# Summing two of four kv batches on another engine, one load for four rows, third buffers, and a planner rule that starts late

## The chip, the cores and the metric

The kernel runs on one core of a Trainium2 chip. A core has TensorE (PE, matmuls), VectorE (DVE), ScalarE (ACT), GpSimd (POOL) and SyncE (SP, which issues most DMAs). The metric is the device time of one execution in microseconds (us).

## The reference

Two layers follow each other. The first is attention with pooled keys; the second a mixture of experts that sends each row to one expert.

```
kv_pool = kv.reshape(4, 96, 4, 8, 4, 128).mean(axis=(2, 4))      # 4 x 4 windows
k = v = kv_pool.reshape(4, 768, 128) @ w_sr
a = softmax(q @ k.T / sqrt(128))                                 # q: 4 x 12288 x 128
x = (a @ v).reshape(49152, 128)
logits = (x / |x|) @ (expert_emb / |expert_emb|).T / tau         # 8 experts
e = argmax(logits); g = softmax(logits)[e]
out[rows of e] = g * (relu(x[rows of e] @ w1[e]) @ w2[e])         # hidden width 1024
```

All inputs and the output are fp32. The kernel computes its large products in fp16 with two halves per number (a rounded high half and the low half that remains), so each product is three matmuls.

## The kernel before, in words

The rows of q are taken in 96 steps of 512 (24 for each batch). A step loads q, scales it, turns it (by PE up to step 28, from step 29 on by a transposing DMA out of a tile q2 that holds both halves, `q_hi`, `q_lo`, `q_turn`), multiplies it with the batch's k into four tiles of 128 x 768 scores (`s_mm`, line 684), takes the row maximum on DVE (`s_max`, line 689) and the exponential on ACT (`s_exp`, line 707). The result p is split into halves phi and plo (`p_hi` on ACT, line 725; `p_lo`, line 735, a subtraction on DVE or POOL), a transposing DMA turns each half (`p_t`, line 759), and PE multiplies with v (`av`, line 780). Some early steps turn p by PE instead (`p_turn`, `p_copy`). After four steps a group of 2048 rows is complete: some 18 small DVE operations make its logits (`g_logits`, lines 839 to 911), ranks and places follow, and POOL scatters the rows into expert order (line 188).

From step 23 on, expert tiles of 512 rows run beside the steps: three matmuls per unit (`l1`, line 1397), relu on ACT (`h_hi`, line 1404), the remainder on DVE (`h_lo`, line 1409), the second product (line 1433), the gate's multiply on DVE (`o_out`, line 1443) and scatters of the output on POOL. The expert weights are split into halves once, in the first stage, with a subtraction on POOL for 14 of 16 (`w_lo`, line 1048), and written to a buffer in DRAM. The expert tiles' buffers come from a pool `wk2`, which is opened when the first stage's pool is closed (`open_experts`).

The pooling of kv is done batch by batch, half a batch ahead. Batch 0 is summed by DVE at the start (`kv_load_0` and what follows). Each of the batches 1 to 3 has 8 windows h of 512 columns; for each, `kv_load` brings four rows of 96 x 512 numbers in two DMAs of 384 KB (line 381), each into one of two buffers `kvt`. POOL adds them in five operations: two rows and two rows (line 390), both sums (line 394), then the four columns in two steps (`kv_cols`, lines 406 and 411), into `pooled`. `kv_t`, `kv_k` and what follows turn the sums and make k and v.

The order of every engine's instructions is not written out: a planner (`Plan`) simulates the engines. Each operation has an engine, an estimated duration, a key (a planned time that serves as its priority), and what it depends on, buffers included: `turn(tag, n)` names the users of the buffer n uses back. In each turn the planner lets the engine that is free first take the ready operation of the lowest key. Operations marked `port=True` have one more rule: one on DVE is not begun while one on POOL is planned to run, nor the reverse. Another ready operation without the mark goes first, or the engine waits. The order that comes out is the order in each engine's queue; on the chip each engine works through its queue in order and waits on semaphores.

The parts that the change touches are: `kv_load`, `kv_rows`, `kv_cols` (lines 379 to 415) and their calls in `kv_ops` (lines 1518 to 1538), the port rule in `Plan.run` (line 295), the buffers of `q2` (line 649), `phi` (line 722) and `plo` (line 732) with their `turn` calls in `step_ops`, and the planned duration of the logits' operations in `group_ops`. A third buffer lets an operation start before the DMA that reads the buffer of two uses ago has landed.

Of the kernel before, what the change touches and what calls it, by code (L numbers as in the profile page):

```python
# [46 lines left out]
    avd=0.262, m=1.928, end=-1.35, ne=-6.946, ge=-32,  # L47
# [4 lines left out]
def attention_moe(  # L52
# [11 lines left out]
    nc = tc.nc  # L64
# [31 lines left out]
    PTB = 4  # L96
    NP = 6
# [119 lines left out]
    class Plan:  # L217
# [33 lines left out]
        def run(self, begin):  # L251
# [18 lines left out]
            while any(count):  # L270
# [24 lines left out]
                if op.port:  # L295
                    other = held["POOL" if eng == "DVE" else "DVE"]
                    if other > t + 0.1:
                        rest = [x for x in now[eng] if not x[2].port and self.can_go(x[2])]
                        if rest:
                            x = min(rest)  # L300
                            now[eng].remove(x)
                            now[eng].append((op.key, i, op))
                            heapq.heapify(now[eng])
                            op = x[2]
                        else:
                            t = other
# [70 lines left out]
    def kv_load(b, h, i):  # L377

        t = kvs.tile([NI, 2, QC], F32, tag="kvt", name=f"kvt{b}_{h}_{i}", bufs=2)
        src = kv[b].rearrange("(i r) w c -> i r (w c)", r=R)  # L380
        nc.sync.dma_start(out=t, in_=src[:, 2 * i : 2 * i + 2, h * QC : (h + 1) * QC])
        st[b]["kvt", h, i] = t

    def kv_rows(b, h, eng):


        def half(i):
            t = st[b].pop(("kvt", h, i))
            st[b]["r", h, i] = kvs.tile([NI, QC], F32, tag=f"kva{i}", name=f"kva{b}_{h}_{i}", bufs=2)
            eng.tensor_tensor(out=st[b]["r", h, i], in0=t[:, 0, :], in1=t[:, 1, :], op=ALU.add)  # L390

        def both():
            r = st[b]["r", h, 0]
            eng.tensor_tensor(out=r, in0=r, in1=st[b].pop(("r", h, 1)), op=ALU.add)

        return [lambda: half(0), lambda: half(1), both]

    def kv_cols(b, h, eng):


        def third():
            if h == 0:
                st[b]["pooled"] = kvs.tile([NI, NJ, C], F32, tag="pooled", name=f"pooled{b}")
            v = st[b].pop(("r", h, 0)).rearrange("p (j r c) -> p j r c", j=JQ, r=R)
            a3 = kvs.tile([NI, JQ, 2, C], F32, tag="kva3", name=f"kvc{b}_{h}", bufs=2)
            eng.tensor_tensor(out=a3, in0=v[:, :, 0:2, :], in1=v[:, :, 2:4, :], op=ALU.add)
            st[b]["a", h] = a3

        def fourth():
            a3 = st[b].pop(("a", h))  # L410
            eng.tensor_tensor(
                out=st[b]["pooled"][:, h * JQ : (h + 1) * JQ, :], in0=a3[:, :, 0, :], in1=a3[:, :, 1, :],
                op=ALU.add,
            )

        return [third, fourth]
# [230 lines left out]
    def q_hi(k):  # L647
        if by_dma(k):
            ks[k]["q2"] = wk.tile([P, NQ, 2, C], F16, tag="q2", name=f"q2_{k}")
# [69 lines left out]
    def p_hi(k, j):  # L719
        h, i = divmod(j, 2)  # L720
        if i == 0:
            ks[k]["h", h] = [wk.tile([P, 2, NK], F16, tag="phi", name=f"phi{k}_{h}")]
# [6 lines left out]
    def p_lo(k, j):  # L729
        h, i = divmod(j, 2)  # L730
        if i == 0:
            ks[k]["h", h].append(wk.tile([P, 2, NK], F16, tag="plo", name=f"plo{k}_{h}"))
# [785 lines left out]
    def kv_ops(b):  # L1518
        mine = [None] * NQR
        for h in range(NQR if b else 0):  # L1520
            t0 = slot(b * SPB, -8 * (X["kv"] - h * X["kvs"]))
            eng, what, ta, tb_ = nc.gpsimd, "POOL", 1.25, 0.7
            rows = kv_rows(b, h, eng)
            parts = []
            for i in range(2):
                o = add("SP", 0.45, t0 + i, lambda h=h, i=i: kv_load(b, h, i), *turn("kvt", 2), dma=1.3, hold=True)
                took("kvt", o)
                r = took(f"kva{i}", add(what, ta, t0 + 8.0 + i * 0.1, rows[i], o, *parts, *turn(f"kva{i}", 2), port=True))
                reads("kvt", r)
                parts.append(r)  # L1530
            r = add(what, ta, t0 + 8.2, rows[2], *parts, port=True)
            reads("kva1", r)
            cols = kv_cols(b, h, eng)
            r = add(what, tb_, t0 + 8.3, cols[0], r, *(turn("pooled", 1) if h == 0 else mine[h - 1 : h]), port=True)
            if h == 0:
                took("pooled", r)
            reads("kva0", r)
            mine[h] = add(what, 0.45, t0 + 8.4, cols[1], r, port=True)
# [99 lines left out]
    x_swap = None  # L1638
    scaled_q = {}
# [3 lines left out]
    def step_ops(k):  # L1643
# [19 lines left out]
        if by_dma(k):  # L1663
            key -= X["ql"]
            hi = took("q2", add("ACT", 0.61, key, lambda: q_hi(k), qa, *turn("q2", 2)))
# [13 lines left out]
        for j in range(NQ):  # L1679
# [16 lines left out]
            if j % 2:  # L1696
# [14 lines left out]
                for i in range(2):  # L1711
                    on = p_mode(k, j - 1 + i)
                    his.append(
                        add(ENG[on[0]], P_HI[on[0]], v + i, lambda j=j, i=i: p_hi(k, j - 1 + i), t_s[k][j - 1 + i], *(his if i else turn("phi", 2)))
                    )
                    if i == 0:
# [4 lines left out]
                            *(los if i else turn("plo", 2)), port=True,  # L1721
# [53 lines left out]
    def group_ops(g, t):  # L1775
        if g == NGRP - 1:
# [3 lines left out]
            t, 0.3, ops, *counted[g], *placed.get(g - 1, ()), *placed.get(g - 2, ()), dur=0.22, port=True,  # L1780
# [61 lines left out]
    x_open = add("-", 0.0, TM[0] - 20.0, open_experts, *stores, *early, v_ready[0])  # L1842

# [77 lines left out]
```

## Time and profile before

| what | value |
|---|---|
| median of 3 runs | 2122.8 us (2112.49 to 2125.25) |
| the profiled execution's own time | 2116.39 us |
| its span, first to last instruction | 2114.4 us |
| mean granted TensorE clock | 0.982 |
| busy: PE, DVE, ACT, POOL | 1954.2 (92%), 1722.0 (81%), 1548.1 (73%), 1323.6 us (63%) |

A row of the profile by stretch gives the busy time of PE, of PE's weight loads, of DVE, ACT and POOL, each with its count of instructions, then the clock that PE was granted (1.00 is 2.4 GHz), and the DMA engines' share. In a timeline a row is the start, the duration, the engine, the line and the operation, its output and inputs; what stands in brackets is the time that the engine idled before it, and whose end ended that. An operation's duration includes time in which it has begun and is held up.

### The profile page before, as it was taken

Reading aid. Unit: us, or ns where it says so; the run is one execution under the profiler, and the core shown is the slowest. Engines: PE = TensorE matmul, PEld = TensorE weight load, DVE = VectorE, ACT = ScalarE, POOL = GpSimd, SP = SyncE. Lnnn points to the kernel's source line nnn. Section 1 sums busy time; section 2 is a strip of 40 time slices with the busy share of each in tenths; the row PEclk is TensorE's granted clock in tenths of the full one; section 3 lists DMA queues with packets and bytes.
Section 4 is the critical chain, followed back from the end, with each engine's and each line's share of the span. In section 5 each row is a group of like instructions: output and inputs, shape, how many; then the busy total and the mean of one; then the engine's idle time right before and its main releaser. Section 6 shows DMA issues by size and latency. Waiting matters only on the chain. (4 is left out here: it accounts for less than half of the span.)

```text
span 2114.4 us, 57446 instructions
## 1 busy us (share of the span) xinstructions
PE 1954.2 (92%) x21396; PEld 1502.7 (71%) x21396; DVE 1722.0 (81%) x3679; ACT 1548.1 (73%) x3256; POOL 1323.6 (63%) x1824
## 2 busy tenths in 40 slices
PE   3777888799999999999999999899999999999998
PEld 2556666567777777677777777677777777777797
DVE  7887788598889899789889888788888888766565
ACT  3886789578787878787787888788888887744443
POOL 1547544468777876577876675566576577567443
PEclk9998999999999999999999999999999999999999
DMA  8977445889898998979898988979888888623242
GB/s 245 205 195 183 124 109 124 182 167 164 165 167 160 190 178 159 209 138 178 169 179 141 167 163 149 190 146 160 147 165 143 156 160 139 119 61 82 57 92 78
DMA packets 844925, 322.64 MB, mean 153 GB/s; under 512 B 793042, under 2 KB 804443, under 8 KB 842848
## 3 DMA queue, kind: packets, MB, share of 16 engines
q1 hardware_dynamic: 817568, 264.13, 66.8%
q0 software_dynamic: 24704, 53.53, 9.7%
q8 instruction: 170, 2.79, 0.5%
q10 hardware_dynamic: 2368, 1.25, 0.2%
q14 instruction: 115, 0.94, 0.2%
HBM read 170.55 MB, written 64.50 MB: 111 GB/s over the span
## 5 line engine op out<-in xcount | busy, mean ns | idle before, releaser
L1409 DVE SCALAR_TENSOR_TENSOR hl<-ph,hh 128x512 f16<-128x512 f32 x740 | 506.8, 686 | 185.7 <-ACT hh L1404 178.3
L188 POOL DMA_INDIRECT out_dram<-o,m x388 | 411.1, 1060 | 325.7 <-DVE o L1443 112.0
L1404 ACT ACTIVATE hh<-ph 128x512 f16<-128x512 f32 x740 | 440.5, 595 | 237.8 <-PE ph L1397 178.8
L1397 PE MATMUL ph<-x,wbuf 128*128 128x512 f16 (+1 forms) x2328 | 600.1, 370 | 8.9 <-DVE hl L1409 6.6
L188 POOL DMA_INDIRECT xs_rows<-rows,pi x384 | 417.7, 1088 | 146.4 <-issue 110.9
L1433 PE MATMUL po<-wbuf,hh 128*128 128x128 f16 x5920 | 453.5, 220 | 30.1 <-DVE o L1443 14.7
L684 PE MATMUL s<-k,qT 128*128 128x512 f16 (+1 forms) x2304 | 442.9, 332 | 30.6 <-ACT p L707 23.1
L707 ACT ACTIVATE p<-s,nm,qa 128x768 f32<-128x768 f32 x384 | 379.9, 990 | 83.3 <-DVE nm L701 75.9
L1433 PEld LDWEIGHTS <-hh 128*128 128x128 f16 x6208 | 383.5, 98 | 52.7 <-issue 23.0
L689 DVE TENSOR_REDUCE nm<-s 128x1 f32<-128x768 f32 x384 | 364.1, 948 | 25.2 <-PE s L684 23.3
L735 DVE TENSOR_TENSOR plo<-p,phi 128x768 f16<-128x768 f32 x339 | 340.8, 1006 | 29.4 <-ACT phi L725 19.0
L684 PEld LDWEIGHTS <-qT 128*128 128x128 f16 x2304 | 219.4, 99 | 165.7 <-issue 44.9
L780 PE MATMUL xp<-v,pthi 128*128 128x137 f16 x4200 | 314.6, 225 | 13.8 <-DVE w L567 5.4
L1397 PEld LDWEIGHTS <-wbuf 128*128 128x128 f16 x2544 | 226.2, 98 | 127.7 <-issue 13.7
L780 PEld LDWEIGHTS <-pthi 128*128 128x128 f16 x4200 | 276.7, 98 | 50.9 <-issue 17.0
L1433 PEld LDWEIGHTS <-hl 128*128 128x128 f16 x3104 | 228.9, 98 | 111.2 <-issue 1.7
L725 ACT CAST phi<-p 128x768 f16<-128x768 f32 x345 | 287.2, 834 | 13.7 <-DMA pthi<-phi 9.3
L1433 PE MATMUL po<-wbuf,hl 128*128 128x128 f16 x2960 | 286.4, 219 | 0.0
L780 PE MATMUL xp<-v,ptlo 128*128 128x137 f16 x2100 | 188.7, 226 | 0.0
L780 PEld LDWEIGHTS <-ptlo 128*128 128x128 f16 x2100 | 143.5, 98 | 0.0
L813 POOL TENSOR_TENSOR rows<-x,rows 128x512 f16<-128x512 f32 x96 | 111.7, 1164 | 25.7 <-ACT rows L808 25.4
L828 ACT ACTIVATE junk<-x 128x128 f32<-128x128 f32 x384 | 116.7, 312 | 13.5 <-DVE x L801 13.5
(359 smaller groups left out, 2004.7 us busy)
## 6 DMA issues: line engine op xcount, KB each, us to landing
wbuf<-w_prep SPq DMA_DIRECT2D x106, 1026.0 KB
kvt<-in_kv_dram SPq DMA_DIRECT2D x64, 384.0 KB
q<-in_q_dram SPq DMA_DIRECT2D x96, 256.0 KB
wf<-in_moe_w_dram SPq DMA_DIRECT2D x16, 512.0 KB
out_dram<-o,m POOLq DMA_INDIRECT x388
xs_rows<-rows,pi POOLq DMA_INDIRECT x384
w_prep<-wo SPq DMA_DIRECT2D x8, 514.0 KB
w_prep<-wo SPq DMA_DIRECT2D x8, 512.0 KB
```

The costliest lines, as they stand in the source:

```text
L188: ins = nc.gpsimd.indirect_dma_start(out=dst[:, :], out_offset=bass.IndirectOffsetOnAxis(ap=idx, axis=0), in_=src, in_offset=None, bounds_ ...
L684: nc.tensor.matmul(t[:, lo:hi], qs[:, l, :], r[:, lo:hi], start=i == 0, stop=i == 2)
L689: V.tensor_reduce(out=nm, in_=ks[k]["s", j], axis=AX.X, op=ALU.max, negate=True)
L707: nc.scalar.activation(out=p, in_=ks[k].pop(("s", j)), func=AF.Exp, bias=ks[k].pop(("nm", j)), scale=ks[k]["fac"],)
L725: nc.scalar.copy(out=hi, in_=p)
L735: eng.tensor_tensor(out=lo, in0=ks[k].pop(("p", j)), in1=hi, op=ALU.subtract)
L780: nc.tensor.matmul(ks[k]["xp", h][:, i, :w], l[:, c, :], r[:, c, :w], start=n == 0, stop=n == len(terms) - 1)
L828: nc.scalar.activation(out=junk, in_=ks[k]["x"][:, j, 0:C], func=AF.Square, accum_out=groups[g]["ss"][:, i * NQ + j : i * NQ + j + 1],)
L1397: nc.tensor.matmul(ph[:, kk * n : (kk + 1) * n], wt[:, o + f : o + f + P], r, start=i == 0, stop=i == 2)
L1404: nc.scalar.activation(out=hh, in_=ts[t]["ph", u], func=AF.Relu)
L1409: V.scalar_tensor_tensor(out=hl, in0=ts[t].pop(("ph", u)), scalar=0.0, in1=ts[t]["hh", u], op0=ALU.max, op1=ALU.subtract)
L1433: nc.tensor.matmul(ts[t]["po"][:, j * C : (j + 1) * C], h[:, kk * n + j * P : kk * n + (j + 1) * P], wt[:, f : f + P], start=u == 0 and i ...
```

## The change

The windows of batches 2 and 3 are summed by DVE: two reductions per window, each over rows and columns at once (16 numbers, 512 bytes apart) for 64 of the 128 channels. Batch 1 stays with POOL, whose five adds now work in place in the loaded tile. One DMA of 768 KB loads the four rows of a window, again with two buffers. The port rule holds only from the planner's time 350 on. The halves phi and plo have three buffers each instead of two. The tile q2 has three buffers instead of two and lies in `wk2`, so its steps wait for `open_experts`. The planned duration of the logits' operations is 0.17 instead of 0.22 for groups 0 to 3.

```diff
-    avd=0.262, m=1.928, end=-1.35, ne=-6.946, ge=-32,
+    avd=0.262, m=1.928, end=-1.35, ne=-6.946, ge=-32, pt=350.0, kd=(2, 3),
...
+    PB = 3
+    Q2 = 3
...
-                if op.port:
+                if op.port and t > X["pt"]:
...
+    def kv_load(b, h):
+        t = kvs.tile([NI, R, QC], F32, tag="kvt", name=f"kvt{b}_{h}", bufs=2)
+        nc.sync.dma_start(
+            out=t, in_=kv[b].rearrange("(i r) w c -> i r (w c)", r=R)[:, :, h * QC : (h + 1) * QC]
+        )
+        st[b]["kvt", h] = t
...
+        return [
+            lambda: add(row(0), row(0), row(1)), lambda: add(row(2), row(2), row(3)),
+            lambda: add(row(0), row(0), row(2)), lambda: add(cols(0, 2), cols(0, 2), cols(2, 4)),
+            lambda: add(lambda: kv_pooled(b, h), cols(0, 1), cols(1, 2)),
+        ]
+
+    def kv_window(b, h, i):
+        if i == 0:
+            kv_pooled(b, h)
+        c = slice(i * C // 2, (i + 1) * C // 2)
+        V.tensor_reduce(
+            out=st[b]["pooled"][:, h, c], in_=st[b]["kvt", h].rearrange("p r (w c) -> p c r w", w=R)[:, c],
+            axis=AX.XY, op=ALU.add,
+        )
...
-            ks[k]["q2"] = wk.tile([P, NQ, 2, C], F16, tag="q2", name=f"q2_{k}")
+            ks[k]["q2"] = wk2.tile([P, NQ, 2, C], F16, tag="q2", name=f"q2_{k}", bufs=Q2)
...
-            ks[k]["h", h] = [wk.tile([P, 2, NK], F16, tag="phi", name=f"phi{k}_{h}")]
+            ks[k]["h", h] = [wk.tile([P, 2, NK], F16, tag="phi", name=f"phi{k}_{h}", bufs=PB)]
...
-            ks[k]["h", h].append(wk.tile([P, 2, NK], F16, tag="plo", name=f"plo{k}_{h}"))
+            ks[k]["h", h].append(wk.tile([P, 2, NK], F16, tag="plo", name=f"plo{k}_{h}", bufs=PB))
...
+            o = took("kvt", add("SP", 0.45, t0, lambda h=h: kv_load(b, h), *turn("kvt", 2), dma=2.6, hold=True))
+            deps = turn("pooled", 1) if h == 0 else mine[h - 1 : h]
+            r = None
+            if b in X["kd"]:
+                for i in range(2):
+                    r = add("DVE", 1.2, t0 + 8.0 + 0.2 * i, lambda h=h, i=i: kv_window(b, h, i), o, r, *deps)
+                    reads("kvt", r)
+            else:
+                for i, (fn, dur) in enumerate(zip(kv_adds(b, h), (1.25, 1.25, 1.25, 0.7, 0.45))):
+                    r = add("POOL", dur, t0 + 8.0 + 0.1 * i, fn, o, r, *deps, port=True)
+                    reads("kvt", r)
...
-            hi = took("q2", add("ACT", 0.61, key, lambda: q_hi(k), qa, *turn("q2", 2)))
+            hi = took("q2", add("ACT", 0.61, key, lambda: q_hi(k), qa, *turn("q2", Q2)))
+            opened.append(hi)
...
-            t, 0.3, ops, *counted[g], *placed.get(g - 1, ()), *placed.get(g - 2, ()), dur=0.22, port=True,
+            t, 0.3, ops, *counted[g], *placed.get(g - 1, ()), *placed.get(g - 2, ()), dur=0.22 if g > 3 else 0.17, port=True,
...
+    for o in opened:
+        o.left += 1
+        x_open.users.append(o)
```

## Rows read from the trace of the kernel before

**Rows 1.** Busy time of every engine by stretch: busy us (instructions), PEclk, DMA share, GB/s

```profile
45.00:130.00 85.00, 66.86 (x605) 50.19 (x604) 71.06 (x149) 70.65 (x142) 38.45 (x31) 0.94 0.85 196
...
130.00:260.00 130.00, 100.20 (x762) 80.95 (x762) 102.09 (x217) 91.29 (x184) 86.77 (x91) 0.88 0.68 171
...
260.00:400.00 140.00, 112.60 (x952) 88.22 (x951) 106.89 (x262) 107.77 (x229) 64.11 (x100) 0.94 0.55 124
...
400.00:450.00 50.00, 42.14 (x413) 29.91 (x413) 37.63 (x69) 31.11 (x69) 27.85 (x42) 0.97 0.88 186
...
450.00:1150.00 700.00, 676.44 (x7663) 513.59 (x7661) 619.29 (x1305) 554.90 (x1198) 516.90 (x720) 1.00 0.90 169
...
1150.00:1850.00 700.00, 691.03 (x7895) 527.62 (x7894) 597.53 (x1306) 563.36 (x1207) 451.91 (x652) 1.00 0.85 155
```

**Rows 2.** PE's waits from 450 to 1150 us: us in total, times, longest

```profile
PE po L1433 <- DVE o L1443: 8.7, 10, 3.0
...
PE po L1433 <- ACT hh L1404: 7.7, 6, 4.2
```

**Rows 3.** Timelines of DVE, POOL and PE: start, us, engine, line, operation [idle before]

```profile
429.22 3.05 DVE L851 TENSOR_TENSOR n4z<-y 128x16 f32<-128x16 f32 x1
...
429.74 2.49 POOL L390 TENSOR_TENSOR kva<-kvt 96x512 f32<-96x512 f32 x2
...
432.93 1.35 PE L1397 MATMUL ph<-x,wbuf 128*128 128x512 f16 x3 [2.15 <-DVE hl L1409]
...
643.42 3.79 DVE L618 TENSOR_SCALAR qa<-qa 128x2 int32<-128x2 int32 x1
...
643.49 2.48 POOL L390 TENSOR_TENSOR kva<-kvt 96x512 f32<-96x512 f32 x2
...
648.80 1.01 PE L1433 MATMUL po<-wbuf,hh 128*128 128x128 f16 x8 [2.97 <-DVE o L1443]
...
741.68 1.22 DVE L618 TENSOR_SCALAR qa<-qa 128x2 int32<-128x2 int32 x1
```

**Rows 4.** Timelines of ACT and PE around the late relu

```profile
859.09 0.72 ACT L650 ACTIVATE q<-q,qa 128x512 f16<-128x512 f32 x1 [3.99 <-DMA qT<-q]
...
860.35 1.03 PE L1433 MATMUL po<-wbuf,hh 128*128 128x128 f16 x8 [4.17 <-ACT hh L1404]
...
1355.19 1.03 PE L1433 MATMUL po<-wbuf,hh 128*128 128x128 f16 x8 [4.09 <-ACT hh L1404]
```

**Rows 5.** Groups by line, POOL, 400 to 1150 us: busy us, mean ns

```profile
L390 POOL TENSOR_TENSOR kva<-kvt 96x512 f32<-96x512 f32 x32 | 40.7, 1283 | 6.1 <-DMA kvt<-in_kv_dram 6.1
```

**Rows 6.** Single lines, whole run: ns min/median/max, first and last start

```profile
L1007 DVE TENSOR_REDUCE wm<-wf x16: 1196/1206/1219, 35.7 to 219.9; 128x1 f32<-128x1024 f32 x16
...
L650 ACT ACTIVATE q<-q,qa x67: 707/721/761, 453.9 to 1760.0; 128x512 f16<-128x512 f32 x67
...
L381 SPq DMA_DIRECT2D kvt<-in_kv_dram x48: 312/393/1195, 122.0 to 1070.3; - x48
```

**Rows 7.** Waits of all engines from 40 to 400 us

```profile
PE s L684 <- ACT p L707: 22.2, 20, 2.9
...
PE s L369 <- ACT p L707: 17.6, 16, 2.6
...
ACT phi L725 <- DMA pthi<-phi: 5.4, 1, 5.4
```

**Rows 8.** Timelines of DVE, POOL and PE in the first stage

```profile
129.44 4.45 DVE L854 SCALAR_TENSOR_TENSOR n0z<-n0z,ss 128x16 f32<-128x16 f32 x1
...
272.23 4.58 DVE L632 TENSOR_SCALAR qa<-qa,ksc 128x2 f32<-128x2 f32 x1
...
272.57 4.21 POOL L1048 TENSOR_TENSOR wo<-wf,wo 128x1024 f16<-128x1024 f32 x2
...
278.41 0.87 PE L369 MATMUL pp<-ident,pooled 96*128 96x96 f32 x4 [5.17 <-DVE nm L701]
```

**Rows 9.** Groups by line, POOL, 45 to 400 us

```profile
L188 POOL DMA_INDIRECT xs_rows<-rows,pi x56 | 59.6, 1065 | 23.6 <-issue 15.4 <-DVE rows L976 5.3 <-DVE nm L701 2.3
```

More of the change, by code (lines that the diff above doesn't have):

```diff
@@ L375, in attention_moe @@
     st = [dict() for _ in range(B)]
[L377 to L416, printed above, removed]
+    def kv_load(b, h):
[4 more added lines that the diff above has]
+        st[b]["kvt", h] = t
@@ new lines, in kv_pooled, with kv_adds, add, row @@
+    def kv_pooled(b, h):
+        if h == 0:
+            st[b]["pooled"] = kvs.tile([NI, NJ, C], F32, tag="pooled", name=f"pooled{b}")
+        return st[b]["pooled"][:, h, :]
+    def kv_adds(b, h):
+        def add(out, in0, in1):
+            nc.gpsimd.tensor_tensor(out=out(), in0=in0(), in1=in1(), op=ALU.add)
+        def row(i):
+            return lambda: st[b]["kvt", h][:, i, :]
+        def cols(lo, hi):
+            return lambda: st[b]["kvt", h][:, 0, lo * C : hi * C]
+        return [
[3 more added lines that the diff above has]
+        ]
@@ L1521, in kv_ops @@
             t0 = slot(b * SPB, -8 * (X["kv"] - h * X["kvs"]))
[L1522 to L1534, printed above, removed]
+            o = took("kvt", add("SP", 0.45, t0, lambda h=h: kv_load(b, h), *turn("kvt", 2), dma=2.6, hold=True))
[9 more added lines that the diff above has]
+                    reads("kvt", r)
             if h == 0:
                 took("pooled", r)
-            reads("kva0", r)
-            mine[h] = add(what, 0.45, t0 + 8.4, cols[1], r, port=True)
+            mine[h] = r
         copies = []
@@ L1638, in attention_moe @@
     x_swap = None
+    opened = []
     scaled_q = {}
@@ L1713, in step_ops @@
                     his.append(
-                        add(ENG[on[0]], P_HI[on[0]], v + i, lambda j=j, i=i: p_hi(k, j - 1 + i), t_s[k][j - 1 + i], *(his if i else turn("phi", 2)))
+                        add(ENG[on[0]], P_HI[on[0]], v + i, lambda j=j, i=i: p_hi(k, j - 1 + i), t_s[k][j - 1 + i], *(his if i else turn("phi", PB)))
                     )
@@ L1720, in step_ops @@
                             ENG[on[1]], P_LO[on[1]], v + i + 0.5, lambda j=j, i=i: p_lo(k, j - 1 + i), his[i],
-                            *(los if i else turn("plo", 2)), port=True,
+                            *(los if i else turn("plo", PB)), port=True,
                         )
```

## The prediction

> **What bounds the kernel now.** The busy times by stretch come first [rows 1]. The reader is to see three stages. From 45 to 400 us PE is busy 66.86 + 100.20 + 112.60 = 279.7 of 355 us at a granted clock of 0.88 to 0.94, and no other engine is near full either (DVE 280, ACT 270): this stage, the attention steps that run before any expert tile, is bound by waits between engines. From 450 to 1850 PE is busy over 96% at a clock of 1.00: PE is the bound, and only its idle time can be won. What comes after 1850 the change does not touch. So the change can take time away in two places: the 75 us that PE idles from 45 to 400, and the 7.9 + 23.6 + 9.0 us that it idles from 400 to 1850. A change that only lightens POOL or DVE is worth nothing by itself; it has to end a wait of PE.
>
> Next I read the two stretches of 700 us against each other [rows 1]. They do the same work per step, but the batch sums of batches 2 and 3 lie almost wholly in the first. There POOL is busy 65 us more, DVE 21.8 us more, and PE idles 23.6 instead of 9.0 us. The list of PE's waits in the first one says for whom: 8.7 us for DVE's last multiply of an expert tile, 7.7 us for ACT's relu [rows 2].
>
> Then the timeline around the longest of these [rows 3]. At 643.42 a DVE operation on no more than 128x2 numbers takes 3.79 us. It stands beside POOL adds of kv rows that run from 643.49 on, two in one row of the timeline and a third behind them, and ends with the third. Behind it in DVE's queue stands the multiply of an expert tile, and PE waits 2.97 us for that. At 429.22 a 128x16 operation takes 3.05 us beside two such adds, and PE waits 2.15 us. So a POOL add and a DVE operation that reads SBUF twice, or in its fast form, do not run together, and the loser holds up its whole queue. A block of 1.22 us, at 741.68, was followed by no wait of PE.
>
> The second kind of wait is at 860.35 and 1355.19 [rows 4]: PE waits 4.17 and 4.09 us for a relu, and in front of the first ACT waited 3.99 us in the scaling of q for a transposing DMA to release one of the two q2 buffers (the second is preceded by the same row, with 4.52 us).
>
> **The change, part by part.**
>
> *POOL's sums of batches 2 and 3 go.* The adds of single rows alone are 32 operations and 40.7 us [rows 5]; with the other three kinds POOL is busy the 65 us longer. POOL is no bound (517 of 700 us), so this is worth only what it blocked. The difference in PE's idle time between the two stretches is 14.6 us, and the wait at 432.93 lies ahead of them: 2.15 us. Together 16.7 us at most; at the least nothing, if each wait comes back elsewhere.
>
> *DVE's reductions come.* Two for each of 8 windows of two batches: 32, each reading 96 x 1024 numbers. The nearest row is the DVE reduction over 1024 numbers of SBUF, 1206 ns, with a spread of 1196 to 1219 over 16 of them, so nothing of POOL's held one up [rows 6]. I take 1.2 us: 32 x 1.2 = 38.4 us. DVE gets back about the 21.8 us that it is busy longer in the first stretch. So it goes from 619 to 636 of 700 us: fuller, but not the bound. Below 1.2 us one can hardly come, since that row reads as many numbers side by side; the trace has no wide stride of that size, and I bound it above by twice the row, 2.4 us. The reductions have late keys, so the planner lets them into gaps of DVE, but what comes ready during one waits for its end: relu remainders, maxima, the multiply of a tile. A block of 1.22 us cost PE nothing [rows 3]. I take 0.2 us of PE each, 6.4 us; at 2.4 us a block is close to those that cost PE 2 us, and I take 1 us each, 32 us, for the far end.
>
> *A third q2 buffer.* It ends the waits of 4.17 and 4.09 us, 8.3 us, if the DMA that is late is no later than a step; otherwise nothing. I take 8.3. Moving the tile into the pool that opens with the experts makes these steps wait for that opening; the first of them scales its q at 453.9 us [rows 6], when expert tiles already run (the wait at 432.93 is in one) [rows 3]. That costs nothing.
>
> *Third buffers for the split halves of p.* In the first stage ACT waits 5.4 us for a transposing DMA to give a buffer back [rows 7]. The ends for PE are 0 and 5.4 us; I take 3, because ACT's work is on the way to PE's waits for p there.
>
> *One load for four rows.* 24 issues of SP in place of 48, each 393 ns in the middle [rows 6]: 9.4 us less in SP's queue, where the transposing DMAs of p, q and x stand behind them. In return a load is twice as long and holds its buffer until the last add has read it. Both buffers now hold a whole window, so POOL's first add is less often late. From -2 to +2 us; I take 0.
>
> *The port rule from 350 on only.* Until then the planner orders DVE and POOL by key alone. Nothing on the chip changes by that, only the order of the queues. The rule's present worth can be seen in what still goes wrong: at 272.23 a DVE operation takes 4.58 us and PE waits 5.17 us behind it; at 129.44 one takes 4.45 us [rows 8]. POOL is busy 38.45 + 86.77 + 64.11 = 189.3 of 355 us there [rows 1], and without its scatters, 59.6 us [rows 9], 130 us, 37%. In that stage DVE has by the code some 170 operations that can collide: some 50 low halves of p, about 22 for each of four groups, and scalings of q and w. Met at random, each loses half a POOL operation (half of the 1.28 us of a kv add [rows 5] or of the 2.1 us of a weight's low half [rows 8], an estimated 0.8 us) in 37% of the cases: 170 x 0.37 x 0.8 = 50 us of DVE. Blocks like the two just named already hold a part of that, so the rule prevents a part, not all. Against it: without the rule no urgent operation is put behind a less urgent one, and 39.8 us of PE's waits here are for p from ACT, which hangs on DVE's maxima [rows 7]. The ends are -20 us (half of those waits) and +50 us (all collisions new, all passed on). I take 0.
>
> **The sum.** For 400 to 1850: -16.7 - 8.3 + 6.4 = -18.6, of which I count 15, since a tile that is no longer late for one reason is partly late for the next. With -3 for the buffers of p that is -18. The profiled execution took 2116.4 us (span 2114.4): 2116.4 - 18 = 2098. The median of the runs shown, 2122.8, is 6 us above that execution, and 2098 is 1.2% below the median. About 1%, 21 us, is what a measurement of this kernel can tell from no change.
>
> **The rivals.**
> A. The forecast: 2098, its own range 2086 to 2110.
> B. The first stage shortens too: the order by key alone brings p earlier, and half of PE's waits for it go. For it: no engine is full there, and 39.8 us of waits have one cause [rows 7]. Against it: the longest waits there are collisions, which it does not prevent. 2098 - 20 = 2078.
> C. The reductions are slow: reading numbers 512 bytes apart takes 2.4 us each, DVE is at 636 + 38 = 674 of 700 us, and PE pays 32 instead of 6 us. 2098 + 26 = 2124. For it: no row of before reads so. Against it: the planner is given 1.2 us.
> The Trainium skill speaks for C ("SBUF — State Buffer", section "Door 1: The DMA port swizzle (why [64,N] ≈ [32,N])", the note on cachelines): SBUF is read in lines of 16 bytes, and a read pattern that takes only one number of each line is slowed. By this rule the 32 reductions cost more than the row of contiguous reading; no run here shows it yet.
> D. The other side: without the rule the first stage collides more. Place: 45 to 400 us. Price: up to 50 us, and PE takes nearly all of a long block, as at 272.23 [rows 8]. It decides from the point where it eats the 18 us won: half the price gives 2123, the whole 2148; I take 2135. For it: two blocks of over 4 us stand there even with the rule [rows 8]. Against it: the planner's times there are wrong enough that the rule already misses most of what it is for.
> E. The waits are only moved: POOL's x halves and the selects still block DVE as they do from 1150 to 1850, and what PE gains it loses at the next late relu. 2114.
>
> **How the numbers follow.** Chances: A 0.42, B 0.20, C 0.10, D 0.18, E 0.10. Faster by over 1% (below 2101.6): 0.27 of A and B, 0.47. Slower by over 1% (above 2144): 0.13 of D's, 0.02 each of C and E, 0.17. The rest, 0.36, lies within 1%. The range 2070 to 2138 leaves out the low half of B and the far end of D.
>
> **What would show it right or wrong.** Right: no DVE operation above 3 us between 430 and 1150; PE's idle time from 450 to 1150 down from 23.6 to about 10 us; the two waits near 860 and 1355 gone; 32 reductions of 1.2 us; POOL busy some 80 us less and DVE about as busy as before; first expert tile within 10 us of 400. Wrong: reductions near 2.4 us (C); the first expert tile 20 us later with DVE blocks of several us ahead of it (D), or 20 us earlier (B); PE's idle time after 450 unchanged with other names on the waits (E).

## The result and the profile after

| what | before | after |
|---|---|---|
| median of 6 runs each | 2117.99 us (2112.49 to 2125.25) | 2087.15 us (2085.79 to 2092.09) |
| the profiled execution's own time | 2116.39 us | 2092.09 us |
| its span | 2114.4 us | 2090.0 us |
| first expert tile begins (PE, first `l1`) | 399.4 us | 376.1 us |
| from there to the end | 1715.0 us | 1713.9 us |
| PE's busy time ahead of that tile | 291.8 us | 281.7 us |
| first scores of step 24 begin | 409.8 us | 392.0 us |
| from there to the first scores of step 95 | 1405.5 us | 1395.9 us |
| from there to the end | 299.1 us | 302.2 us |

The changed kernel is faster: 0.9857 of the time before, interval 0.9834 to 0.988. Execution against execution it gains 24.3 us where 18 were forecast; the medians lie 30.8 us apart, and what the medians have more stands in no trace. Where were the 24.3 us won? The first expert tile comes 23.3 us sooner, and from there on both kernels take the same time to within 1.1 us. But that tile is not the same point of the work in both: the changed kernel begins it with PE 10 us less far in its work. The first scores of step 24 are nearly the same point (2455 and 2443 of PE's 21396 matmuls stand ahead of them). Up to there 17.8 us are won, from there to step 95 another 9.6, and behind that 3.0 are lost. PE's idle time agrees. In all it falls from 160.2 to 141.0 us: by 12.0 from 45 to 400 us and by 9.3 from 400 to 1850, while it grows by 2.0 in the rest. The remaining 5.2 us are PE's busy time, which is shorter for as many matmuls. The forecast had put 15 of its 18 us into the stretch from 400 to 1850, and 3 ahead of it.

Busy times of the changed kernel by stretch (PE, PE's weight loads, DVE, ACT, POOL, then clock and DMA), as in [rows 1]:

```profile
45.00:130.00 85.00, 67.07 (x604) 50.66 (x604) 72.27 (x142) 69.50 (x140) 39.10 (x29) 0.94 0.89 202
130.00:260.00 130.00, 103.14 (x801) 80.72 (x800) 112.22 (x227) 95.43 (x196) 97.56 (x100) 0.89 0.71 175
260.00:400.00 140.00, 121.42 (x1060) 95.14 (x1060) 120.84 (x294) 113.00 (x249) 73.07 (x120) 0.94 0.62 132
400.00:450.00 50.00, 46.63 (x520) 35.63 (x519) 39.44 (x87) 38.78 (x85) 35.62 (x56) 0.97 0.97 185
450.00:1150.00 700.00, 679.49 (x7694) 516.73 (x7693) 637.03 (x1331) 561.94 (x1198) 444.02 (x629) 1.00 0.94 173
1150.00:1850.00 700.00, 692.75 (x7933) 529.17 (x7931) 593.47 (x1285) 556.11 (x1198) 444.45 (x648) 1.00 0.82 149
```

PE idles 63.4 instead of 75.3 us from 45 to 400, 3.4 instead of 7.9 from 400 to 450, and 7.2 instead of 9.0 from 1150 to 1850. In the long stretch from 450 to 1150, where POOL's sums had stood, it still idles 20.5 of 23.6 us; POOL is 73 us less busy there and DVE 17.7 us more.

PE's waits of the changed kernel from 450 to 1150 (total us, times, longest), against [rows 2]:

```profile
PE po L1434 <- ACT hh L1405: 7.0, 9, 3.7
PE ph L1398 <- DVE hl L1410: 5.5, 10, 2.2
PE po L1434 <- DVE o L1444: 5.1, 6, 1.6
```

The wait for DVE's multiply falls from 8.7 to 5.1 us. In its place the wait for the relu's remainder, 1.7 us before (third in that list of the kernel before: 3 times, longest 0.9), is 5.5. The timeline shows what stands ahead of one of these:

```profile
657.97 1.88 DVE L414 TENSOR_REDUCE pooled<-kvt 96x64 f32<-96x1024 f32 x1
...
659.78 0.67 DVE L1410 SCALAR_TENSOR_TENSOR hl<-ph,hh 128x512 f16<-128x512 f32 x1
...
660.50 1.44 PE L1398 MATMUL ph<-x,wbuf 128*128 128x512 f16 x3 [2.21 <-DVE hl L1410]
```

A reduction of 1.88 us is in DVE's queue just before the remainder, and PE idles 2.21 us for it. All 32 take that long; the rows of the tile `kvt` give ns as least/median/greatest:

```profile
L382 SPq DMA_DIRECT2D kvt<-in_kv_dram x24: 570/635/1179, 117.5 to 993.5; - x24
L414 DVE TENSOR_REDUCE pooled<-kvt x32: 1876/1920/1955, 489.0 to 1055.4; 96x64 f32<-96x1024 f32 x32
```

The second kind of wait that the forecast ended, [rows 4], is still there, though the one of 4.09 us near 1355 is gone (PE's waits for the relu from 1150 to 1850 fall from 4.4 to 0.5 us). ACT's waits in q's scaling for the transposing DMA from 450 to 1900 are 16.5 us, against 14.7 before, and one of them ends as at 860 before:

```profile
853.87 0.72 ACT L651 ACTIVATE q<-q,qa 128x512 f16<-128x512 f32 x1 [4.84 <-DMA qT<-q]
854.49 0.58 ACT L1405 ACTIVATE hh<-ph 128x512 f16<-128x512 f32 x1
...
855.13 1.04 PE L1434 MATMUL po<-wbuf,hh 128*128 128x128 f16 x8 [3.71 <-ACT hh L1405]
```

A count in the trace says why. Before, q's scaling had run one step ahead of the transposing DMA in 66 of 67 cases; now it runs two ahead in 63 of 67. The planner, told of three buffers, filled the third at once.

So what made the first expert tile come sooner? It is not in [rows 7]: the scores of step 23 begin no sooner, and PE's waits for p from 45 to 400 went from 39.8 to 34.1 us only.

```profile
PE s L685 <- ACT p L708: 24.5, 19, 4.5
PE s L371 <- ACT p L708: 9.6, 6, 3.1
```

The traces point to another chain. By the code (`open_experts`) the expert tiles' buffers take the place of the first stage's pool, which closes when the last tile of unsplit p in it has been used: PE's last product `xp<-v,pw`, of step 20. Not before that can SP load the first weights and rows. In the kernel before (timelines of DVE, PE, SP and POOL from the same stretch):

```profile
356.81 0.30 DVE L911 TENSOR_TENSOR oh<-iom,mx 128x128 f16<-128x128 f32 x1
...
378.94 0.17 PE L925 MATMUL rk<-ones,oh 128*128 128x1 f16 x1
...
381.71 0.20 POOL L1130 TENSOR_TENSOR t_cnt<-base,basec 128x8 f32<-128x8 f32 x1 [22.19 <-DVE base L946]
...
382.09 1.54 PE L780 MATMUL xp<-v,pthi 128*128 128x137 f16 x12 [1.06 <-DVE qa L618]
...
385.62 1.43 SPq L759 DMA_TRANSPOSE pthi<-phi  x1
...
386.94 3.05 PE L772 MATMUL xp<-v,pw 128*128 128x137 f32 x24 [1.02 <-DVE t_st L1205]
...
392.22 0.39 SPq L1360 DMA_DIRECT2D wbuf<-w_prep  x1
393.63 2.60 SPq L1371 DMA_TRANSPOSE x<-xs_rows  x2
...
399.38 0.59 PE L1397 MATMUL ph<-x,wbuf 128*128 128x512 f16 x2
```

and in the changed kernel:

```profile
335.79 0.29 DVE L912 TENSOR_TENSOR oh<-iom,mx 128x128 f16<-128x128 f32 x1
...
336.13 0.18 PE L926 MATMUL rk<-ones,oh 128*128 128x1 f16 x1
...
360.74 3.05 PE L773 MATMUL xp<-v,pw 128*128 128x137 f32 x24
...
362.83 1.42 SPq L760 DMA_TRANSPOSE pthi<-phi  x1
...
366.44 0.37 SPq L1361 DMA_DIRECT2D wbuf<-w_prep  x1
367.83 2.58 SPq L1372 DMA_TRANSPOSE x<-xs_rows  x2
...
376.07 1.36 PE L1398 MATMUL ph<-x,wbuf 128*128 128x512 f16 x3
```

That last unsplit product, the gate from here on, ends at 390.0 before and at 363.8 after; the first load follows 2 to 3 us behind it in both. What SP waits for last is not the gate, though. Before, SP stands from 375.5 to 385.6 for PE's product of split p at 382.09, which gives a buffer of turned p back, and then issues four transfers ahead of the load; after, the transfer ahead of the load starts at 362.83, when ACT has made that half of p. The steps of q are no faster up to there: the scores of step 23 begin at 371 and 372 us. What differs is the order of PE's queue. Before, PE works from 353 to 379 us almost on scores alone, most of them waiting for ACT's exponential, and behind them stand the rank `rk` of the fourth group (whose one-hot had been ready at 357.1, 22 us earlier; POOL idles 22.19 us for what follows from it), two products of split p (`pthi`, `ptlo`), and the gate. After, the rank runs at 336.13, right behind its one-hot, and the products are done among the scores.

PE takes its queue in order, so a rank that comes late makes both late that stand behind it, the product that SP waits for and the gate. DVE's operations for the logits ahead of that rank carry the mark `port=True`: some 20 of them, mostly 0.15 to 0.3 us long, take 16.6 us before (from 340.26, between maxima and halves of p) and 9.8 after (from 326.04). So the late rule bears on this chain. Whether it is the cause was the question for the runs.

### The profile page after: what moved, and what is told of

Its sections match the earlier page's. It is cut to its first block, busy times and chain, and to the rows that moved or that the text cites. A ratio compares the mean times of both kernels' runs of the same rounds, so it can differ in the third digit from the quotient of the medians.

```text
span 2090.0 us, 57341 instructions
## 1 busy us (share of the span) xinstructions
PE 1949.0 (93%) x21396; PEld 1499.7 (72%) x21396; DVE 1748.6 (84%) x3711; ACT 1550.2 (74%) x3256; POOL 1253.1 (60%) x1744
## 5 line engine op out<-in xcount | busy, mean ns | idle before, releaser
L690 DVE TENSOR_REDUCE nm<-s 128x1 f32<-128x768 f32 x384 | 364.4, 949 | 21.2 <-PE s L685 17.8
L736 DVE TENSOR_TENSOR plo<-p,phi 128x768 f16<-128x768 f32 x339 | 349.4, 1031 | 16.8 <-ACT phi L726 13.9
## 6 DMA issues: line engine op xcount, KB each, us to landing
kvt<-in_kv_dram SPq DMA_DIRECT2D x16, 384.0 KB
```

What stands on the lines that cost most here:

```text
L690: V.tensor_reduce(out=nm, in_=ks[k]["s", j], axis=AX.X, op=ALU.max, negate=True)
L736: eng.tensor_tensor(out=lo, in0=ks[k].pop(("p", j)), in1=hi, op=ALU.subtract)
```

## The experiments

The twelve runs came in three sets of four, on three chips that all run this program slower than the chip of the two profiles: the kernel before takes 2313 to 2323 us there. Operations are as long as before (the relu 597 ns in both profiles of the changed kernel), but PE idles more in the expert tiles, and a new kind of gap has no releaser in the trace ("issue"). PE's waits from 450 to 1150 in the control `after_again`:

```profile
PE po L1434 <- ACT hh L1405: 12.9, 16, 1.9
PE po L1434 <- issue: 8.6, 16, 1.7
PE ph L1398 <- DVE hl L1410: 6.6, 12, 1.5
```

What these gaps are stays open. So times are compared as ratios to the kernel before on the same chip, and places by the instants of the chain above. One limit holds for all that follows: the changed kernel itself was run again in the second set alone, so a ratio of the first or third set has its control on another chip. All of them at a glance (us; "rest" is the span less the first tile, "24 to 95" the time between the first scores of these steps; the two profiles stand on top):

| kernel | median | ratio to before | `rk` on PE | gate ends | first tile | rest | step 24 | 24 to 95 |
|---|---|---|---|---|---|---|---|---|
| before | 2117.99 | | 378.9 | 390.0 | 399.4 | 1715.0 | 409.8 | 1405.5 |
| after | 2087.15 | 0.9857 | 336.1 | 363.8 | 376.1 | 1713.9 | 392.0 | 1395.9 |
| **first set** (before: 2323.25) | | | | | | | | |
| rule_always | 2279.72 | 0.9813 (0.9758 to 0.9867) | 375.6 | 387.6 | 395.0 | 1889 | 413.2 | 1515 |
| pool_all | 2277.47 | 0.9828 (0.9772 to 0.9885) | 344.2 | 371.8 | 384.0 | 1881 | 401.1 | 1510 |
| two_p_bufs | 2274.51 | 0.9807 (0.9755 to 0.9858) | 343.5 | 377.5 | 390.3 | 1876 | 406.5 | 1506 |
| two_q2_bufs | 2271.02 | 0.9771 (0.9716 to 0.9827) | 344.1 | 371.8 | 384.2 | 1888 | 400.5 | 1513 |
| **second set** (before: 2315.9) | | | | | | | | |
| after_again | 2259.09 | 0.9745 (0.971 to 0.978) | 342.3 | 370.0 | 382.3 | 1867 | 398.7 | 1493 |
| before_rule_late | 2269.8 | 0.9797 (0.9763 to 0.9831) | 360.0 | 368.3 | 378.8 | 1875 | 399.7 | 1501 |
| rule_never | 2294.41 | 0.9891 (0.9849 to 0.9933) | 339.6 | 367.3 | 379.6 | 1915 | 396.2 | 1535 |
| side_by_side | 2262.02 | 0.977 (0.9719 to 0.9822) | 341.0 | 369.1 | 381.4 | 1857 | 397.9 | 1480 |
| **third set** (before: 2313.43) | | | | | | | | |
| before_again | 2311.56 (one run) | | 391.2 | 402.5 | 414.3 | 1895 | 425.3 | 1528 |
| sums_alone | 2286.56 | 0.9872 (0.9822 to 0.9922) | 374.8 | 390.5 | 404.5 | 1887 | 417.0 | 1513 |
| q2_planned_two | 2267.98 | 0.9798 (0.9781 to 0.9814) | 345.5 | 373.2 | 385.6 | 1904 | 401.9 | 1532 |
| dve_tree | 2252.03 | 0.9737 (0.971 to 0.9764) | 340.1 | 367.8 | 380.2 | 1870 | 396.7 | 1496 |

In all fourteen traces the first load of weights is issued 0 to 4.4 us after the gate's end and the first tile begins 7 to 14 us after it, so the gate holds as a mark in time. As the thing that SP waits for it shows in two of them only, `before_rule_late` and `two_p_bufs`, where the load is issued 0.04 us after its end; in the others SP's queue comes to the load later. On these chips one kernel's runs lie up to 29 us apart (`side_by_side`: 2240.04 to 2269.46, and a fourth at 2273.7), so the columns "rest" and "24 to 95", from one execution each, tell nothing below some 20 us; the instants in the first 400 us are steadier: in the control and the six kernels that differ from it only later, the gate ends between 367.3 and 373.2.

**The controls.**

> The changed kernel itself once more, as a control beside the three others of this set and, if the chip is a slower one, for the first four runs: a ratio of 0.983 to 0.989 to the kernel before. It says nothing on the theories; it says whether the ratio carries from one chip to another.

> The kernel before itself, as a control with a trace, for the sets that run on chips slower than that of the two profiles. Theory S: its step 24 begins 10 to 18 us later than in the two kernels that differ from it by the late rule (399 to 400 us there), and from step 24 to step 95 it takes some 10 to 25 us more than the changed kernel's 1492 us in the same set. If the late rule's gain on such chips lies after 400 us instead, step 24 begins within 5 us of theirs.

The ratio does not carry: the change is worth 2.55% on the second set's chip, outside the 0.983 to 0.989 expected, and 1.43% on the chip of the two profiles. What carries is the chain: on the slower chips the first tile is 32 us sooner (414.3 to 382.3, from one chip to another), on the first chip 23 us. Step 24 begins at 425 us in `before_again`, at 399 in `after_again` and 400 in `before_rule_late`: in the first stage, as theory S has it, only by 26 us and not 10 to 18. From step 24 to 95 `before_again` takes 1528 us, 36 more than the changed kernel, more than was foreseen. In these single executions more than half of the gain lies behind step 24; the first stage is the whole of it neither here nor on the first chip.

**The port rule alone, and undone.**

```diff
 before_rule_late (on the kernel before)
-    ... ge=-32,
+    ... ge=-32, pt=350.0,
-                if op.port:
+                if op.port and t > X["pt"]:
 rule_always (on the changed kernel)
-    pt=350.0
+    pt=-1000.0
 rule_never (on the changed kernel)
-    pt=350.0
+    pt=1e9
```

> The kernel before with the port rule from 350 on only, nothing else of the change. Theory S (the gain sits in the first stage, and the late rule is the larger part of it, since an operation is no longer put behind less urgent ones): the first expert tile 10 to 15 us sooner than in the kernel before (399 us), the DVE blocks from 450 to 1150 as before, ratio 0.993 to 0.996. Rival M (the gain comes from the POOL blocks that went in the middle, and from the buffers): first expert tile within 4 us of 399, ratio 0.998 to 1.002. Rival D of the forecast (without the rule the first stage collides more): ratio above 1.003.

> The changed kernel with the port rule on from the start, all else as changed. Changed: 2087 us, before: 2118 us; step 24 begins at 392 us in the changed kernel and at 410 us before. Theory 1 (the first stage won the time, by the order without the rule): most of the 18 us comes back, some 2103 to 2108 us, step 24 near 410, DVE's port waits from 45 to 400 us down from 45 towards 32 us. Theory 2 (the time was won after 400 us, by the POOL sums that no longer block DVE): 2085 to 2092 us.

Timelines of `before_rule_late`:

```profile
359.95 0.17 PE L925 MATMUL rk<-ones,oh 128*128 128x1 f16 x1
...
365.23 3.02 PE L772 MATMUL xp<-v,pw 128*128 128x137 f32 x24
...
378.80 0.81 PE L1397 MATMUL ph<-x,wbuf 128*128 128x512 f16 x3 [2.22 <-DVE qT L664]
```

and of `rule_always`:

```profile
375.60 0.16 PE L926 MATMUL rk<-ones,oh 128*128 128x1 f16 x1 [0.43 <-DVE v L568]
...
384.52 3.08 PE L773 MATMUL xp<-v,pw 128*128 128x137 f32 x24 [0.32 <-ACT x L800]
...
394.95 1.38 PE L1398 MATMUL ph<-x,wbuf 128*128 128x512 f16 x5 [2.25 <-DMA x<-xs_rows]
```

The late rule and nothing else brings the rank 31 us, the gate 34 us and the first tile 35 us forward (to 378.8 from 414.3; the two traces are of two chips), and is worth 2.0% where the whole change, on the same chip, is worth 2.55%. The expected 10 to 15 us and 0.4 to 0.7% were too small. Not all of it lies ahead of the tiles: step 24 comes 26 us sooner, and from there to step 95 the two traces differ by another 27. Taking the late rule out of the full change puts the rank back by 33 us, the gate by 18 and the first tile by 13 (31, 16 and 11 against `two_q2_bufs` on its own chip), with a ratio of 0.9813. That is 0.0068 above the control's, with an uncertainty of 0.0065 (the root of the sum of the squared half intervals). Against `two_q2_bufs` the medians are 8.7 us apart and the runs overlap slightly, so this loss is not well resolved. Both directions agree in place and sign: in the first stage the rule had held the chain back. They do not add up (2.0% alone, 0.7% when removed), since other parts of the change bring the gate forward too. Where the rule is in force from the start, the gate begins 8 to 13 us behind the rank (the two kernels before, `rule_always`, `sums_alone`); in the control it is 25 us, so there the rank no longer decides. That the planner puts the marked operations behind others for POOL's sake and so plans the rank later is read from the code; no run shows the planner's own times. How an earlier rank and first tile shorten the time behind step 24 is not shown either.

What the rule had been for is cheap there. DVE's time above its usual lengths from 45 to 400 us (each operation against the lower quartile of its kind, what is under 0.04 us left out) is 32 us in `before_rule_late`, as in `before_again`, and 42 in the control against 28 in `rule_always`: 14 us of DVE, not the 50 of rival D, in a stage where DVE has gaps. From 400 to 1150 it is 38 us in `before_rule_late` against 50 in `before_again`, so the blocks there did not stay quite as before.

> The changed kernel with the port rule at no time. Theory S (order by key alone is enough in the first stage because PE, DVE and POOL all have gaps there; after 400 us PE is the bound and DVE's queue is nearly full, so each collision is paid): DVE's excess from 400 to 1850 two to four times the 33 us of the changed kernel, several DVE operations above 3 us after 430 us, 10 to 30 us longer than the changed kernel. Rival U (the rule is useless throughout, the planner's times are too wrong for it): within 4 us of the changed kernel or shorter.

Without the rule after 350 us too, the kernel loses 1.5% to the control of the same set (0.9891 against 0.9745), 35 us where 10 to 30 were expected, although its first tile is even sooner. So theory U falls. But the reason that theory S gave is not what the trace shows: no DVE operation exceeds 2.7 us after 430, and DVE's time above usual lengths from 400 to 1850 is 29 against 22 us. PE's waits from 400 to 1850 grow under these names, here `rule_never`:

```profile
PE po L1434 <- ACT hh L1405: 35.0, 35, 3.5
...
PE po L1434 <- DVE o L1444: 16.4, 15, 5.2
```

against 22.3 and 12.9 us in the control. That the order, rather than collisions, makes the relu late is a guess; it wasn't tried.

**The sums, alone and undone.**

```diff
 sums_alone (on the changed kernel)
-    pt=350.0
+    pt=-1000.0
-    PB = 3
-    Q2 = 3
+    PB = 2
+    Q2 = 2
 pool_all (on the changed kernel)
-    kd=(2, 3)
+    kd=()
```

> The kernel before with the sums of batches 2 and 3 on DVE, the one load for four rows, the place of q2 and the logits' planned duration; the port rule is in force throughout and every buffer is a pair, as before. Theory A of the forecast for the sums (POOL's blocks of 14 to 17 us go, 6 to 10 come with the reductions): 5 to 12 us shorter than before, ratio 0.994 to 0.998. Theory S, where the first stage holds the gain: the same on that point, but step 24 within 4 us of the kernel before. Rival (the reductions of 1.9 us cost PE as much as the POOL blocks did): ratio 0.998 to 1.005.

> The changed kernel with batches 2 and 3 summed by POOL again (five adds in place, one load). Theory 1: within 6 us of 2087. Theory 2: 2100 to 2110 us, with DVE operations held over 3 us beside POOL's adds between 430 and 1150 us again, and PE's idle time from 450 to 1150 us up from 20.5 us. If the reductions of 1.92 us cost as much as the blocks did, the time is the same or even lower by some us.

`sums_alone` gains 1.3%, more than any of its expectations, and 10 of its 18 us of span (2309.6 to 2291.3) come before the first tile, against the expectation that step 24 would stay: it begins at 417 instead of 425 us. The rank comes 16 us sooner than in `before_again` and the gate 12:

```profile
374.82 0.17 PE L926 MATMUL rk<-ones,oh 128*128 128x1 f16 x1
...
387.46 3.04 PE L773 MATMUL xp<-v,pw 128*128 128x137 f32 x24
...
404.54 1.46 PE L1398 MATMUL ph<-x,wbuf 128*128 128x512 f16 x6
```

Of its edits the logits' shorter planned duration is the nearest cause for another place of the rank; it wasn't tried by itself. With the sums back on POOL and all the rest kept, the ratio is 0.9828, 0.0083 above that of the control on the other chip, with an uncertainty of 0.0066 made up in the same way; the first tile, at 384.0 us, is within 2 us of the control's. DVE's time above usual lengths from 400 to 1150 is 38 us there against 11, so blocks do come back, though none above 2.4 us; it is 50 in `before_again`. Whether PE pays for them is open. Against `two_q2_bufs`, on the same chip, the medians are 6.5 us apart and the runs overlap (2266.78 to 2287.67 and 2260.9 to 2273.41); PE idles 61.3 instead of 48.8 us from 450 to 1150, but 38.0 instead of 50.9 from 1150 to 1850. On the chip of the two profiles the 9.3 us of idle time that went between 400 and 1850 were not taken apart.

**What a reduction costs.**

```diff
 side_by_side (on the changed kernel)
-            ... .rearrange("p r (w c) -> p c r w", w=R)[:, c],
+            ... .rearrange("p r (w c) -> p (r w c)", w=R)[:, i * 1024 : (i + 1) * 1024].rearrange("p (c r w) -> p c r w", r=R, w=R),
 dve_tree (on the changed kernel)
...                                                     # kv_tree: four adds of DVE in place
-                for i in range(2):
-                    r = add("DVE", 1.2, t0 + 8.0 + 0.2 * i, lambda h=h, i=i: kv_window(b, h, i), o, r, *deps)
+                for i, (fn, dur) in enumerate(zip(kv_tree(b, h), (1.15, 0.62, 0.35, 0.22))):
+                    r = add("DVE", dur, t0 + 8.0 + 0.1 * i, fn, o, r, *deps, port=True)
```

> The changed kernel with the 32 reductions reading 1024 numbers that lie side by side instead of 512 bytes apart (same count, same output size, same order; what is summed is another set of numbers, so pooled, and all that follows from batches 2 and 3, is left out of account). If the stride is what makes a reduction 1.92 us: 1.2 us each, 23 us less DVE from 430 to 1150. Theory P (PE pays for a reduction about 0.2 us): 3 to 7 us shorter than the changed kernel. Rival H (the reductions lie in DVE's gaps and cost PE nothing): within 2 us. If the reduction over two axes is slow by itself, it stays at 1.9 us.

> The changed kernel with each window of batches 2 and 3 summed by four adds of DVE in place (1024, 512, 256 and 128 columns, all reading side by side, under the port rule) instead of two strided reductions. By the rows of such adds at the start of the changed kernel (1.22 us for 1024, 0.69 for 512, 0.42 for 256) 2.6 us a window instead of 3.8: 19 us less DVE. If DVE's length of queue is what PE pays for: 3 to 8 us shorter. If collisions decide (adds with two operands in SBUF stand against POOL's, reductions don't): blocks above 2 us come back and it is 3 to 10 us longer.

The reduction over side-by-side numbers, from the groups by line of `side_by_side` (busy us, mean ns):

```profile
L414 DVE TENSOR_REDUCE pooled<-kvt 96x64 f32<-96x1024 f32 x32 | 38.5, 1202 | 0.0
```

The stride alone makes 1202 into 1918 ns, a factor of 1.6; the two-axis form by itself costs nothing. The Trainium skill's rule on cachelines ("SBUF — State Buffer", section "Door 1: The DMA port swizzle (why `[64,N]` ≈ `[32,N]`)") says that a read which crosses to a new line with each number is slowed; the trace agrees, with these two durations. But no gain shows: 23 us less DVE time give 0.977 against 0.9745 on the same chip. The four runs of `side_by_side` lie far apart; without the longest their mean is 2254.7 us against 2257.9 in the control. A gain of 3 to 7 us, as theory P had it, is below what these runs resolve. The tree of four adds tells the same story from the other side:

```profile
L415 DVE TENSOR_TENSOR kvt<-kvt 96x1024 f32<-96x1024 f32 (+2 forms) x48 | 38.7, 806 | 0.0
L415 DVE TENSOR_TENSOR pooled<-kvt 96x128 f32<-96x128 f32 x16 | 5.7, 358 | 0.1
```

44.4 us in place of 61.4, the longest DVE operation after 430 us 2.5 us long (2.7 in the control), and 0.9737 against 0.9745 (on another chip): no difference. Single waits like that at 660.50 exist, but DVE's 17 to 23 us are not on the path to the end in any amount that these runs resolve.

**The buffers.**

```diff
 two_p_bufs (on the changed kernel)
-    PB = 3
+    PB = 2
 two_q2_bufs (on the changed kernel)
-    Q2 = 3
+    Q2 = 2
 q2_planned_two (on the changed kernel: three buffers, planned as two)
-            hi = took("q2", add("ACT", 0.61, key, lambda: q_hi(k), qa, *turn("q2", Q2)))
+            hi = took("q2", add("ACT", 0.61, key, lambda: q_hi(k), qa, *turn("q2", 2)))
```

> The changed kernel with two buffers each for phi and plo, as before. If the third buffers bring the first stage forward (theory 3): step 24 later by 10 us or more, 2097 us or more. If they do little (theories 1 and 2): 2084 to 2092 us.

With a pair for each half of p the rank comes as early as in the control, but the gate ends 7.5 us and the first tile begins 8 us later:

```profile
374.43 3.02 PE L773 MATMUL xp<-v,pw 128*128 128x137 f32 x24
...
390.32 1.02 PE L1398 MATMUL ph<-x,wbuf 128*128 128x512 f16 x4 [2.73 <-ACT x L800]
```

Against `two_q2_bufs`, on the same chip, it is 6 us for each, and step 24 is 6 us later, not the 10 that the theory asked for. Here SP does stand at the first load until the gate ends. The gate's input is p, so p is the likely cause of its lateness. The ratio is 0.9807, 0.0062 above the control's on the other chip (uncertainty 0.0062) and 0.0036 above that of `two_q2_bufs` (0.0075). So the place is shown, and the size of the term of 3 us is not contradicted.

> The changed kernel with two buffers for q2 (still in the later pool). In the changed kernel ACT still waits 16.5 us for the DMA that turns q2 (14.7 before), and q is scaled two steps ahead of that DMA instead of one: the planner filled the third buffer at once. By that the third buffer is worth nothing: 2084 to 2090 us, ACT's wait again some 15 us, its lead one step. By the prediction's step (8 us won): 2095 us.

> The changed kernel with three q2 buffers, but the planner orders the steps as if there were two, so that the third is a reserve on the chip and not an earlier place in ACT's queue. Theory L (the planner filled the third buffer at once: the scaling of q runs two steps ahead of the transposing DMA instead of one, and so waits for the buffer as before): ACT's waits in the scaling for the transposing DMA fall from 4 to 16 us to under 1 us, and the time is 0 to 6 us shorter than the changed kernel. Rival (the DMA is late because of its own queue, and nobody behind it is on PE's path): waits as before, or gone with the time the same within 3 us.

Two q2 buffers give 0.9771, not to be told from the control's 0.9745: no gain of 8 us is seen from the third. But on these chips the wait is small to begin with: 3.1 us in `before_again`, 4.1 in the control, 4.5 with two buffers, where the chip of the profiles has 14.7 and 16.5. `q2_planned_two` is the cleaner test. ACT's waits for the transposing DMA are gone from its list, just as theory L said, and yet the kernel is not shorter but 0.5% longer than the control on the other chip, with intervals that do not overlap. So theory L is right about the wait, and the 0 to 6 us that it promised did not come; that the wait is a symptom of ACT being early, and that it would be worth as little on the first chip, is not shown.

## Why the prediction was right, and where it was not

The time and the direction held: 2092.09 us for the profiled execution against 2098, and 2087.15 for the median, near the lower end of A's own range of 2086 to 2110. The way there did not hold: the forecast took 15 us from the stretch from 400 to 1850 and 3 from the first stage, and PE's idle time fell by 9.3 and 12.0. That the total came close is luck in part: one share was too large and the other too small.

- **POOL's sums, -16.7 us.** The blocks went as foreseen: DVE's time above usual lengths from 400 to 1150 fell from 61.9 to 12.0 us, and no DVE operation between 430 and 1150 exceeds 3 us. PE's time did not follow as forecast: its idle time from 450 to 1150 was to fall from 23.6 to about 10 us and fell to 20.5. The step that failed is the reading of the 14.6 us difference in PE's idle time as the price of the blocks; with the 4.5 us from 400 to 450, PE's idle time fell by 7.6 us up to 1150, the reductions paid, and `pool_all` does not resolve how much of that the blocks were. For the long stretch rival E was nearer: most of the waits moved to other names.
- **The reductions, +6.4 us.** Mis-sized per piece: 1.92 us, not 1.2, between the forecast and rival C, 61.4 us in all and not 38.4. What PE pays for them stays below what the runs resolve: `side_by_side` and `dve_tree` take 23 and 17 us of DVE out and no gain is seen, so rival C's price of 32 us is not borne out. DVE's 637 us in the long stretch equals the forecast's 636 by two errors that cancel: 44 us came back (61.4 less the 17.7 that DVE is busier) in place of 21.8.
- **The third q2 buffer, -8.3 us.** Failed in the main. Of the two waits the one of 4.09 us is gone and the one of 4.17 is still 3.71. The condition, that the late DMA be "no later than a step", overlooked that the planner decides who uses the buffer; it let ACT run one step further ahead, and ACT's wait stayed at 16.5 us. Where such waits were really removed, on a chip where they come to some 3 us (`before_again`), nothing was gained.
- **Third buffers of p, -3 us.** Right in place; the first tile is 6 to 8 us later without them, and the time is within the intervals.
- **One load for four rows, 0 us.** An issue of the larger load takes 635 ns and not 393, so SP's queue is 3.6 us shorter and not 9.4. Its worth was not tried by itself.
- **The port rule, 0 us.** The main miss. The ends named were -20 and +50; on a slower chip the late rule alone is worth 46 us, beyond the lower end, and 13 us of the first tile in the full change. On the chip of the forecast it was not run alone. Rival B had the place (before 400 us) and its sign, and its 2078 lies 14 us from the profiled execution, but its mechanism, p coming earlier, accounts for a part at most: the waits for p lost 5.7 of 39.8 us, not half. The forecast counted the logits' operations among the 170 that can collide and did not ask what stands behind the last of them. The waits of [rows 7] are the largest of PE's and so drew the eye; what told of the late rank was one wait of POOL, 22.19 us, left unread because POOL is no bound, and what told of the expert tiles' late start was their first row, read only as a date.
- **The signs named in advance** caught it: "first expert tile within 10 us of 400" was false at 376.1, "20 us earlier (B)" was close, and of the two waits near 860 and 1355 one stayed.

## What to carry to other kernels

When a stage runs with every engine half idle, look for the one event that lets the bound engine's work begin, and follow the chain behind it through all engines, the idle waits of a lightly used one included; here 17.8 of 24.3 us were won ahead of step 24. Measure such a gain between points that mean the same work in both kernels: by the first expert tile nothing seemed won behind it, by the steps 9.6 us were. A rule that orders queues to avoid collisions can cost more than the collisions: here it held back, in a stage with gaps, what everything waits for, and paid for itself only later (1.5%, `rule_never`). A buffer that a planner knows of need not be slack: here it was filled in 63 of 67 steps, and a wait that disappears proves nothing until the time moves.

## What the runs showed that was not expected

A reduction on DVE over 1024 fp32 numbers per partition takes 1.92 us at 512 bytes apart and 1.20 us side by side. On three of the four chips PE has gaps that end with no releaser in the trace, up to 28.6 us in total under one name from 400 to 1850 us in `before_again` (none on the first chip), and the kernel before takes 9% more there with operations of the same length; the same change is worth 2.55% on one of them and 1.43% on the first chip. What those gaps are was not found.
